# Shifting the SBUF start addresses of a two-layer network's matmul operands by 64 bytes

## The chip, the cores and the metric

The kernel runs on one core of one Trainium2 chip. The metric is the device time of one execution in microseconds, the median of three runs. "Moving" is the operand that streams through TensorE, "stationary" the one that a weight load (LDWEIGHTS) places in the array before the matmul. All sizes and offsets are per SBUF partition; an offset means start address modulo 128 bytes.

## The reference

```python
def reference(...):
    x = attention in chunks of 64 over q, k, v            # (8, 8, 576, 64)
    x = _moe_ref(x.transpose(...).reshape(8, 576, 512), ...)  # causal attention of 4 experts, 2 chosen
    return _moe2_ref(x, g_ln, w_ch1, w_ch2)

def _moe2_ref(x, g_ln, w_ch1, w_ch2):                     # "the second network"
    mu = np.mean(x, axis=-1, keepdims=True)
    var = np.mean((x - mu) ** 2, axis=-1, keepdims=True)
    xn = (x - mu) / np.sqrt(var + 1e-06) * g_ln
    ch = np.maximum(xn @ w_ch1, 0.0) @ w_ch2              # 512 -> 2048 -> 512 for 4608 rows
    return (x + ch).astype(np.float32)
```

## The kernel before, in words

The first 447 us are the two attentions; the change leaves their matmuls alone. After them the second network runs as two matrix products, one after the other, each by a Strassen-like scheme of seven products on quarter blocks. Every fp32 operand is split into a high and a low part, so that each product takes three matmuls (stationary high with moving low, low with high, high with high). All 6048 matmuls have a 128x128 stationary and a 128x256 moving operand of type float32r, and each comes with its own weight load.

**First product** (`prod1`, L864, 3024 matmuls, from `group1_steps`). The moving operand is the normalised input, seven tiles `x7_1` to `x7_7` in pool `sx`, made anew for each of nine row blocks j. The stationary operand is a weight chunk `w1u0` to `w1u7`. The loop over `seq` takes four steps d for each j; step d uses chunks 2d and 2d+1. A step issues seven groups of twelve matmuls in the order (1, n), (7, n), (3, n-1), (6, n), (4, n-1), (2, n), (5, n): groups 3 and 4 belong to the step before and use its chunks. Groups 1, 3, 6 and 5 write the bank `bb`, groups 2, 4 and 7 the pair `ad`. In steps 1 and 2 of each j but the last, eight transposes of the next block (`norm`, L802) stand between groups 4 and 2.

**Second product** (`group2`, L1132, 3024 matmuls). Here the weights `w2u1` to `w2u7` move, and the hidden activations are stationary: `his` and `los`, halves of 4 KB that `take()` deals out of a free list of slots left by the first product (`x7_*`, `xc`, `raw64`, `cv`, `cw`, named `hx7_*`, `hxc`, `hraw64`, `hcv`, `hcw` there) and of seven new ones (`n0` to `n6`, later `hn*`). `product` issues low, high, high for each block.

Where a tile lies is set by the pools: they are stacked from both ends of SBUF, in the order in which they are opened, so a tile's offset follows from the sizes of those before it. In the program before, the offsets of the second network's operands are these two, 64 bytes apart:

```
operand                                        before   after
x7_1 to x7_7          moving, first product        96      32
w1u0 to w1u3          stationary, first            96      96
w1u4 to w1u7          stationary, first            32      96
w2u1, w2u2, w2u5-7    moving, second product       96      32
w2u3, w2u4            moving, second               32      32
hraw64, hcv, hcw, n*, hn*   stationary, second     32      96
hx7_*                 stationary, second           96      96
hxc (two buffers)     stationary, second       96, 32      96

pairs moving/stationary, matmuls   96/96  96/32  32/32  32/96
first product, before               1512   1512      -      -
second product, before               704   1456    488    376
both products, after                   -      -      -   6048
```

The prediction speaks of *same* pairs (96/96 and 32/32) and *crossed* pairs (96/32 and 32/96). The functions that the diff touches:

Of the kernel before, what the change touches and what calls it, by code (L numbers as in the profile page):

```python
# [7 lines left out]
F32 = mybir.dt.float32  # L8
F32R = mybir.dt.float32r
# [13 lines left out]
def tile_kernel(ctx, tc, dims, qkt, vt, wqt, wkt, wvt, wo, g_ln, w_ch1, w_ch2, out):  # L23
    nc = tc.nc
    B, H, S, D = dims
    E, HD, DM = wo.shape
# [13 lines left out]
    VW = NV + E  # L40
# [13 lines left out]

    def f32(ap):
        return ap.bitcast(F32)

    ident = const.tile([128, 128], F32)
    nc.gpsimd.memset(ident, 0.0)
# [7 lines left out]
    sc = ctx.enter_context(tc.tile_pool(name="sc", bufs=1, side="right"))  # L67
    se = early.enter_context(tc.tile_pool(name="se", bufs=1, side="right"))
# [64 lines left out]
    def part_of(n):  # L133
        c, half = n[0], int(n[1])
        if c == "o":
            return woh[:, half, :], wol[:, half, :], wo[2 * half:2 * half + 2].rearrange("e d n -> (e d) n"), None
        hi, lo, src, sc = SRC[c]
        fs = slice(half * 2, half * 2 + 2)
        return hi[:, fs, :], lo[:, fs, :], src[:, fs, :], sc

    held = {}
    PARTS = [c + h for c in "kqvo" for h in "01"]

    def weight_load(n):
        src = part_of(n)[2]
        c, half = n[0], int(n[1])
        if c not in held:
            held[c] = se.tile([128, 4 * VW], F32, name="wraw") if c == "q" else sc.tile([128, 4 * VW], F32, name="xc", bufs=2)
        raw = held[c][:, half * 2 * VW:half * 2 * VW + src.size() // 128]
        if half:  # L150
            held.pop(c)
        if c != "o":
            raw = raw.rearrange("p (a b) -> p a b", a=2)
        nc.sync.dma_start(raw, src)
        raws[n] = raw
# [8 lines left out]
    def weight_low(n, eng):  # L164
        hi, lo, _, sc = part_of(n)
        if sc is None:
            eng.tensor_tensor(lo, raws.pop(n), f32(hi), OP.subtract)
        else:
            eng.scalar_tensor_tensor(lo, raws.pop(n), sc, f32(hi), OP.mult, OP.subtract)
# [50 lines left out]
    def chunk_split(g, acc):  # L220
        gi, j = divmod(g, GT)
        if j == 0:
            groups[gi] = (sp_.tile([128, KF, GW], F32R, name="xTh", bufs=2), sp_.tile([128, KF, GW], F32R, name="xTl", bufs=2))
        cs = slice(j * 128, (j + 1) * 128)
        xh, xl = (x[:, :, cs].rearrange("p f (c i) -> p f c i", c=2) for x in groups[gi])
        src = acc.rearrange("p c f i -> p f c i")
        return (lambda: nc.scalar.activation(xh, src, AF.Copy)), (lambda: nc.vector.tensor_tensor(xl, src, f32(xh), OP.subtract))
# [471 lines left out]
    def start_up(op):  # L699
        c, n = op[0], op[1:]  # L700
        if n in PARTS:
            if c == "c":
                weight_load(n)
            elif c == "h":
                weight_high(n)
            else:
                weight_low(n, nc.vector if c == "l" else nc.gpsimd)
        elif c == "P":
            if not projs:
                projs.append(proj_group(0))  # L710
            high, low = next(projs[0])
            highs.append(high)
            lows.append(low)
        elif c == "a":
            highs.pop(0)()
        elif c == "v":
            lows.pop(0)()
        elif c == "G":
            next(projs.pop(0))
            step(gates[0])  # L720
        elif c == "N":
            chunk_shift(int(n), paired.pop(int(n)))
        elif c == "K":
            paired[n, "k"] = chunk_turn(int(n))
        elif c == "k":
            paired.pop((n, "k"))()
        elif c in "HX":
            paired[int(n)].pop(0)()
        else:
            prologue[c](int(n))  # L730
# [8 lines left out]
    w1u = {}  # L739

    def new_w1(pool, c):
        w1u[c] = pool.tile([128, 2, 2, 7, 128], F32R, name=f"w1u{c}", tag=f"u{c}")

    def load_w1(c):
        nc.sync.dma_start(f32(w1u[c][:, :, 1]), w1d[c])
# [18 lines left out]
    x7, tsum, xt = {}, {}, {}  # L764
# [4 lines left out]


    def norm(j, half):
        xc = sc.tile([128, 4 * VW], F32, name="xc", bufs=2)[:, :2 * DM].rearrange("p (a b) -> p a b", a=2)
        nc.sync.dma_start(xc, xs[2 * j + half])
        yield
        mv = sc.tile([128, 2, 2], F32, name="mv", bufs=2)
        for i in range(2):
            st = sc.tile([128, 6], F32, name="st", bufs=2)
            nc.vector.bn_stats(st, xc[:, i])
            nc.vector.bn_aggr(mv[:, i, :], st)
        ve = sc.tile([128, 2], F32, name="ve", bufs=2)  # L780
        sd = sc.tile([128, 2], F32, name="sd", bufs=2)
        rs = sc.tile([128, 2], F32, name="rs", bufs=2)
        nw = sc.tile([128, 2], F32, name="nw", bufs=2)
        nc.vector.tensor_scalar(ve, mv[:, :, 1], 1e-6, None, OP.add)
        nc.scalar.activation(sd, ve, AF.Sqrt)
        yield
        nc.vector.reciprocal(rs, sd)
        nc.vector.tensor_tensor(nw, rs, rs, OP.mult)
        nc.vector.tensor_tensor(nw, nw, ve, OP.mult)
        nc.vector.tensor_scalar(nw, nw, -0.5, 1.5, OP.mult, OP.add)  # L790
        nc.vector.tensor_tensor(rs, rs, nw, OP.mult)
        for i in range(2):
            nc.vector.tensor_scalar(xc[:, i], xc[:, i], mv[:, i, 0:1], rs[:, i:i + 1], OP.subtract, OP.mult)
        yield
        if half == 0:
            xt[j] = sx.tile([128, 4, KF, 256], F32, name="xt")
        t = xt[j][:, half]
        across.add((j, half))
        tp = pss.tile([128, 2, KF, 128], F32, name="tp2", tag="ps2")
        for i in range(2):  # L800
            for f in range(KF):
                nc.tensor.transpose(tp[:, i, f, :], xc[:, i, f * 128:(f + 1) * 128], ident)  # L802
        nc.scalar.activation(t.rearrange("p f (i n) -> p f i n", i=2), tp.rearrange("p i f n -> p f i n"), AF.Copy)
        yield
# [16 lines left out]
            yield  # L821

    def operand_high(j, i):
        t = x7[j, i] = sx.tile([128, 2, 2, 256], F32R, name=f"x7_{i}")
        nc.scalar.activation(t[:, 0], tsum[i], AF.Copy)  # L825

    def operand_low(j, i, eng=nc.vector):
# [4 lines left out]
    def operand(j, i):  # L832
        operand_high(j, i)
        operand_low(j, i)
# [3 lines left out]
    def begin(op):  # L838
        c, n = op[0], int(op[1])
        eng = nc.gpsimd if op[-1] == "P" else nc.vector  # L840
        if c == "i":
            step(started.setdefault(n, norm(0, n)))
        elif c == "u":
            difference(0, n, eng)
        elif c == "h":
            operand_high(0, n)
        elif c == "l":
            operand_low(0, n, eng)
        elif c == "g":
            w1_high(n, int(op[2]))  # L850
        elif c == "m":
            w1_low(n, int(op[2]), eng)
# [63 lines left out]
    def first_weights():  # L916
        nonlocal w1p, sq
        mids.close()
        w1p = ctx.enter_context(tc.tile_pool(name="w1p", bufs=1, side="right", reuse_waits="tile"))
        for c in range(2):  # L920
            new_w1(w1p, c)
            load_w1(c)
        sq = ctx.enter_context(tc.tile_pool(name="sq", bufs=1, side="right", reuse_waits="tile"))
# [12 lines left out]
    sx = ctx.enter_context(tc.tile_pool(name="sx", bufs=1, side="right", reuse_waits="tile"))  # L936
# [7 lines left out]
    for c in range(2, 4):  # L944
        new_w1(w1r, c)
        load_w1(c)
# [3 lines left out]

    w1q = ctx.enter_context(tc.tile_pool(name="w1q", bufs=1, reuse_waits="tile"))
    cx = ctx.enter_context(tc.tile_pool(name="cx", bufs=1, reuse_waits="tile"))
    low = ExitStack()
    w1z = low.enter_context(tc.tile_pool(name="w1z", bufs=1, reuse_waits="tile"))
    for c in range(4, NC):
        pool = w1q if c < 6 else w1z
        new_w1(pool, c)
        load_w1(c)
        if c == 5:
            released.append(True)  # L960
            while kept:
                store(*kept.pop(0))
# [19 lines left out]
    POOLS = {f"x7_{i}": sx for i in range(1, 8)}  # L982
# [16 lines left out]
    def take():  # L999
        t = free.pop(0)  # L1000
        if t in fresh:
            return t, fresh.pop(t)
        if t == "xc":
            return t, sc.tile([128, 4 * VW], F32R, name="hxc", tag=t, bufs=2)[:, :1024].rearrange("p (a b) -> p a b", a=4)
        return t, POOLS[t].tile([128, 4, 256], F32R, name="h" + t, tag=t)

    def give(h):
        free.append(h[0])
# [178 lines left out]
    for n, (j, d) in enumerate(seq):  # L1187
        if d == 0 and j + 1 < NB:
            nrm = [norm(j + 1, 0), norm(j + 1, 1), sums(j + 1)]
            step(nrm[0])  # L1190
            step(nrm[1])
# [40 lines left out]
    n = len(seq) - 1  # L1232
# [10 lines left out]
    for i in range(7):  # L1243
        t = f"n{i}"
# [94 lines left out]
```

## Time and profile before

| what | value |
|---|---|
| median of three runs | 1183.58 us (1183.41 to 1184.11) |
| span of the profiled execution | 1181.6 us |
| the runs' median less that span (start and end) | 1.98 us |
| PE busy | 1167.0 us, 99% |
| weight loads busy | 1120.1 us, 95% |
| DVE, ACT, POOL busy | 75%, 49%, 23% |
| chain of work that ended last | PE 93%, DVE 4% |

The profiled execution's own time is not among the three; its span lies 1.98 us under their median. A busy PE says little here: matmuls are pipelined, a row of one lasts some 280 ns, and the next one starts less than half of that later. What a matmul costs is the distance from its start to the next start, and that is read from the timeline: its rows merge matmuls of one line with the same names, so the distance between two rows' starts, divided by the matmuls of the first, is the cost of one.

### The profile page before, as it was taken

To read this page: it belongs to the slowest core of one execution; us is meant where nothing else is said; L and a number is where in the kernel's file an instruction comes from. 1 tells how busy PE (TensorE), PEld (TensorE's weight loads), DVE (VectorE), ACT (ScalarE), POOL (GpSimd) and SP (SyncE) were. 2 spreads that over 40 slices of the span, in tenths; PEclk is the share of its full clock that TensorE was granted. 3 is DMA by queue.
4 is the path that set the end of the run, shared out by engine and by line. 5 is a ranking of instruction groups with operands and counts; after the bars stand their busy time and mean duration, and the time that the engine had idled before them with its cause. 6 is when DMAs were issued, how large, how long until landed. Compare 5 with 4: busy or idle time off the path is not lost.

```text
span 1181.6 us, 29119 instructions
## 1 busy us (share of the span) xinstructions
PE 1167.0 (99%) x11840; PEld 1120.1 (95%) x11840; DVE 891.7 (75%) x1830; ACT 579.0 (49%) x1099; POOL 276.9 (23%) x490
## 2 busy tenths in 40 slices
PE   8999999999999999999999999999999999999998
PEld 7889989998998879999999999999999999999998
DVE  6888797879888686975776686457998777877783
ACT  4665665656666585533443333346543334333340
POOL 4544545544553450221211211110000000000000
PEclk9999999999999999999999999999999999999999
DMA  8345343334331136755555545559855454545421
GB/s 310 109 142 178 124 148 131 132 134 150 107 131 62 69 102 241 225 187 173 170 184 185 178 164 176 175 168 320 306 178 170 159 163 153 169 155 167 166 86 45
DMA packets 95509, 191.69 MB, mean 162 GB/s; under 512 B 8592, under 2 KB 41360, under 8 KB 94480
## 3 DMA queue, kind: packets, MB, share of 16 engines
q1 hardware_dynamic: 95376, 189.83, 48.6%
q8 instruction: 93, 1.52, 0.5%
q14 instruction: 40, 0.33, 0.1%
HBM read 118.50 MB, written 71.30 MB: 161 GB/s over the span
## 4 chain that ended last, share of the span: by engine, by line
PE 93%; DVE 4%; ACT 1%; issue 1%; DMA 0%; POOL 0%; DVEq 0%; ACTq 0%; POOLq 0%
PE bb L864 17%; PE bb L1132 17%; PE ad L864 13%; PE ad L1132 11%; PE pp L274 8%; PE pv L301 4%; PE oa_ps L458 4%; PE y_ps L468 4%; PE tp L439 4%; PE sp L388 4%; PE sx_ps L182 1%; PE tp L802 1%; PE pT_ps L208 1%; PE sx_ps L218 1%; DVE P L406 1%; ACT P L411 1%
## 5 line engine op out<-in xcount | busy, mean ns | idle before, releaser
L864 PE MATMUL bb<-x,w1u 128*128 128x256 f32 x1728 | 215.8, 280 | 0.0
L864 PEld LDWEIGHTS bb<-x,w1u 128*128 128x128 f32 x1728 | 209.1, 190 | 0.1
L864 PE MATMUL ad<-x,w1u 128*128 128x256 f32 x1296 | 168.7, 282 | 0.0
L864 PEld LDWEIGHTS ad<-x,w1u 128*128 128x128 f32 x1296 | 159.1, 190 | 0.3 <-issue 0.2
L1132 PE MATMUL bb<-w2u,hn 128*128 128x256 f32 x712 | 121.5, 280 | 0.3 <-DVE hn L1056 0.3
L1132 PEld LDWEIGHTS bb<-w2u,hn 128*128 128x128 f32 x712 | 102.3, 189 | 0.5 <-DVE hn L1056 0.5
L428 POOL TENSOR_SCALAR P<-P,l 128x128 f32<-128x128 f32 (+8 forms) x144 | 88.7, 633 | 42.3 <-DVE l L421 37.6
L1132 PE MATMUL bb<-w2u,hx 128*128 128x256 f32 x464 | 94.5, 282 | 0.0
L411 ACT ACTIVATE P<-P,nm 128x128 f32<-128x128 f32 (+8 forms) x144 | 86.9, 607 | 14.4 <-DVE nm L406 14.4
L513 POOL TENSOR_TENSOR cv<-cv 128x512 f32<-128x512 f32 x16 | 27.1, 1696 | 231.1 <-DVE cv L509 231.1
L1132 PE MATMUL ad<-w2u,hn 128*128 128x256 f32 x472 | 81.1, 280 | 0.0
L543 POOL TENSOR_TENSOR cw<-cw 128x128 f32<-128x128 f32 x128 | 64.3, 522 | 60.7 <-issue 41.1
L1132 PEld LDWEIGHTS bb<-w2u,hx 128*128 128x128 f32 x464 | 74.1, 189 | 0.0
L1132 PE MATMUL ad<-w2u,hx 128*128 128x256 f32 x416 | 73.2, 281 | 0.0
L1132 PEld LDWEIGHTS ad<-w2u,hn 128*128 128x128 f32 x472 | 68.6, 188 | 0.0
L406 DVE CUSTOM_DVE_ANT_0 P<-sp,mcaus 128x128 f32<-128x128 f32 (+7 forms) x128 | 60.2, 517 | 8.4 <-PE sp L388 8.0
L829 DVE TENSOR_TENSOR x<-xt,x 128x512 fp32r<-128x512 f32 x61 | 49.8, 817 | 16.9 <-ACT x L825 16.9
L1132 PEld LDWEIGHTS ad<-w2u,hx 128*128 128x128 f32 x416 | 61.0, 189 | 0.0
L458 PE MATMUL oa_ps<-pTa,vg 128*64 128x128 f32 x928 | 59.6, 278 | 0.5 <-DVE pTa L443 0.3
L202 POOL TENSOR_TENSOR pc<-pc,lc 128x512 f32<-128x512 f32 x35 | 37.5, 1072 | 85.8 <-DVE lc L198 62.9
L439 PE MATMUL tp<-ident,P 128*128 128x128 f32 x464 | 57.4, 274 | 0.0
L458 PEld LDWEIGHTS oa_ps<-pTa,vg 128*64 128x64 f32 x928 | 50.7, 138 | 4.7 <-issue 1.1
(353 smaller groups left out, 2821.4 us busy)
## 6 DMA issues: line engine op xcount, KB each, us to landing
qk<-in_qk SPq DMA_DIRECT2D x35, 512.0 KB, 4.2
raw<-in_w_ch SPq DMA_DIRECT2D x32, 512.0 KB, 3.9
hx<-hd SPq DMA_DIRECT2D x28, 512.0 KB, 4.2
hn<-hd SPq DMA_DIRECT2D x24, 512.0 KB, 4.3
vb<-in_v SPq DMA_DIRECT2D x36, 256.0 KB, 4.3
xs<-y SPq DMA_DIRECT2D x36, 256.0 KB, 2.2
xc<-xs SPq DMA_DIRECT2D x18, 512.0 KB, 4.4
hd<-p SPq DMA_DIRECT2D x36, 256.0 KB, 4.3
```

The source lines that it names most:

```text
L274: nc.tensor.matmul(pp, a[:, f, ws], b_[:, f, :], start=(f == 0 and n == 0), stop=(f == KF - 1 and n == 2))
L301: nc.tensor.matmul(pv, a[:, f, cs], b_[:, f, :], start=(f == 0 and n == 0), stop=(f == KF - 1 and n == 2))
L388: nc.tensor.matmul(sv[:, si, :cn], x[r, ep, qc], y[r, ep, c0:c0 + cn], start=first, stop=last)
L406: nc.vector.tensor_tensor_reduce(dst, src, mk, -1.0, -3.0 * NEG, OP.add, OP.min, nm[:, e2:e2 + 1])
L411: nc.scalar.activation(pe, pe, AF.Exp, bias=nm[:, e2:e2 + 1], scale=-1.0, accum_out=l[:, e2:e2 + 1])
L428: nc.gpsimd.tensor_scalar(pe, pe, sums_[g][:, ep, e2:e2 + 1], 1.0, OP.mult, OP.mult)
L439: nc.tensor.transpose(tp[:, i, :], P[ep][e2][:, kt * 128:(kt + 1) * 128], ident)
L458: nc.tensor.matmul(o_ps[e2 * HD:(e2 + 1) * HD, ep, :], vg[:, gk % GT, e * HD:(e + 1) * HD], pT[:, e * n + kt, :], start=(kt == 0), stop=(k ...
L543: nc.gpsimd.tensor_tensor(w[:, o, :], w[:, x, :], w[:, y, :], op)
L829: eng.tensor_tensor(t[:, 1], tsum[i], f32(t[:, 0]), OP.subtract)
L864: nc.tensor.matmul(out[:, p], w[:, kt, a, WI[i], :], x[:, b_, kt, :], start=(start and p == 0 and kt == 0 and q == 0), stop=False, skip_gr ...
L1132: ins = nc.tensor.matmul(out, x[:, c, ts], w2u[i][:, w, half * 4 + c, :], start=begin and q == 0, stop=False, skip_group_check=True)
```

## The change

It puts every moving operand of the second network at offset 32 and every stationary one at 96. Three tools do it: a gap tile of 64 bytes in a pool (`gap`), a tile made longer (`xc` rounded up to whole 128 bytes, an `x7` slot 128 bytes longer than its data), and a view that starts 64 bytes into its tile (`SHIFT`, 16 elements: `w1u0` to `w1u5`, and the slots of `sx` when they hold activations).

```diff
+    LINE = 128
+    MOVING, STILL = 32, 96
+    SHIFT = (STILL - MOVING) // 4
+    XC = -(-4 * VW * 4 // LINE) * LINE // 4
+    SLOT = 1024 + LINE // 4
+
+    def gap(pool, size, name):
+        pool.tile([128, size // 4], F32, name=name)
...
     def new_w1(pool, c):
-        w1u[c] = pool.tile([128, 2, 2, 7, 128], F32R, name=f"w1u{c}", tag=f"u{c}")
+        at = 0 if c > 5 else SHIFT
+        t = pool.tile([128, at + 3584], F32R, name=f"w1u{c}", tag=f"u{c}")
+        w1u[c] = t[:, at:].rearrange("p (k s i n) -> p k s i n", k=2, s=2, i=7)
...
     def norm(j, half):
-        xc = sc.tile([128, 4 * VW], F32, name="xc", bufs=2)[:, :2 * DM].rearrange("p (a b) -> p a b", a=2)
+        xc = sc.tile([128, XC], F32, name="xc", bufs=2)[:, :2 * DM].rearrange("p (a b) -> p a b", a=2)
...
     def operand_high(j, i):
-        t = x7[j, i] = sx.tile([128, 2, 2, 256], F32R, name=f"x7_{i}")
+        t = x7[j, i] = sx.tile([128, SLOT], F32R, name=f"x7_{i}")[:, :1024].rearrange("p (a k t) -> p a k t", a=2, k=2)
+        if (j, i) == (0, 5):
+            gap(sx, STILL - MOVING, "xgap")
...
     cx = ctx.enter_context(tc.tile_pool(name="cx", bufs=1, reuse_waits="tile"))
+    gap(cx, STILL - MOVING, "cgap")
...
-        return t, POOLS[t].tile([128, 4, 256], F32R, name="h" + t, tag=t)
+        at = SHIFT if POOLS[t] is sx else 0
+        h = POOLS[t].tile([128, at + 1024], F32R, name="h" + t, tag=t)
+        return t, h[:, at:].rearrange("p (a b) -> p a b", a=4)
```

No instruction is added, removed or moved on any engine: each one's sequence is the same in both programs, operation by operation. All semaphore waits are the same but one: the DVE subtraction that makes the low part of the first `x7_7` (`operand_low`, L829) waits for one transfer more of a DMA queue, the load of a `vb` tile of the first attention (L118).

## Rows read from the trace of the kernel before

**Rows 1.** The page: span, busy time of TensorE, chain that ended last.
```profile
span 1181.6 us, 29119 instructions
...
PE 1167.0 (99%) x11840; PEld 1120.1 (95%) x11840; DVE 891.7 (75%) x1830; ACT 579.0 (49%) x1099; POOL 276.9 (23%) x490
...
PE 93%; DVE 4%; ACT 1%; issue 1%; DMA 0%; POOL 0%; DVEq 0%; ACTq 0%; POOLq 0%
```

**Rows 2.** Second network: window, length; PE busy (matmuls); granted clock; DMA share; GB/s.
```profile
447.90:1178.50 730.60, 730.28 (x6223) 1.00 0.55 178
```

**Rows 3.** Waits of PE from 447 us on: total us, times, longest.
```profile
PE bb L1132 <- DVE hn L1056: 0.3, 1, 0.3
```

**Rows 4.** PE's timeline, first product: start us, us, engine, line, operation, names, shapes, count.
```profile
461.99 3.04 PE L864 MATMUL bb<-x,w1u 128*128 128x256 f32 x24
464.87 1.60 PE L864 MATMUL ad<-x,w1u 128*128 128x256 f32 x12
466.31 1.04 PE L802 MATMUL tp<-ident,xc 128*128 128x128 f32 x8
467.11 1.68 PE L864 MATMUL ad<-x,w1u 128*128 128x256 f32 x12
...
471.42 1.52 PE L864 MATMUL ad<-x,w1u 128*128 128x256 f32 x12
472.78 2.96 PE L864 MATMUL bb<-x,w1u 128*128 128x256 f32 x24
...
477.02 1.04 PE L802 MATMUL tp<-ident,xc 128*128 128x128 f32 x8
477.81 1.66 PE L864 MATMUL ad<-x,w1u 128*128 128x256 f32 x12
479.31 2.99 PE L864 MATMUL bb<-x,w1u 128*128 128x256 f32 x24
...
489.20 3.00 PE L864 MATMUL bb<-x,w1u 128*128 128x256 f32 x24
...
508.51 1.68 PE L864 MATMUL ad<-x,w1u 128*128 128x256 f32 x12
```

**Rows 5.** PE's timeline, end of the first product.
```profile
808.77 2.88 PE L864 MATMUL bb<-x,w1u 128*128 128x256 f32 x24
...
818.29 1.52 PE L864 MATMUL bb<-x,w1u 128*128 128x256 f32 x12
```

**Rows 6.** PE's timeline, start of the second product, up to its one wait.
```profile
827.91 5.60 PE L1132 MATMUL aa<-w2u,n 128*128 128x256 f32 x48
833.35 0.28 PE L1132 MATMUL ad<-w2u,hcv 128*128 128x256 f32 x1
...
841.95 0.62 PE L1132 MATMUL bb<-w2u,hn 128*128 128x256 f32 x3 [0.27 <-DVE hn L1056]
```

**Rows 7.** PE's timeline, second product: w2u3 with hn, then w2u4 with hx.
```profile
864.67 3.04 PE L1132 MATMUL bb<-w2u,hn 128*128 128x256 f32 x24
867.54 0.28 PE L1132 MATMUL ad<-w2u,hx 128*128 128x256 f32 x1
...
870.36 2.99 PE L1132 MATMUL ad<-w2u,hx 128*128 128x256 f32 x24
873.19 0.28 PE L1132 MATMUL bb<-w2u,hn 128*128 128x256 f32 x1
```

**Rows 8.** PE's timeline: another run with hx (two of w2u7, then w2u4).
```profile
1104.68 3.25 PE L1132 MATMUL ad<-w2u,hx 128*128 128x256 f32 x27
1107.77 0.40 PE L1132 MATMUL ad<-w2u,hn 128*128 128x256 f32 x2
```

**Rows 9.** PE's timeline: the last matmuls.
```profile
1176.85 1.60 PE L1132 MATMUL dt<-w2u,hn 128*128 128x256 f32 x12
```

**Rows 10.** Loads of vb (first and last issue); DVE's subtractions that make low parts.
```profile
L118 SPq DMA_DIRECT2D vb<-in_v x36: 327/364/1107, 3.6 to 337.8; - x36
...
L829 DVE TENSOR_TENSOR x<-xt,x x61: 670/693/1787, 432.7 to 788.4; 128x512 fp32r<-128x512 f32 x61
```

More of the change, by code (lines that the diff above doesn't have):

```diff
@@ L147, in weight_load @@
         if c not in held:
-            held[c] = se.tile([128, 4 * VW], F32, name="wraw") if c == "q" else sc.tile([128, 4 * VW], F32, name="xc", bufs=2)
+            held[c] = se.tile([128, 4 * VW], F32, name="wraw") if c == "q" else sc.tile([128, XC], F32, name="xc", bufs=2)
         raw = held[c][:, half * 2 * VW:half * 2 * VW + src.size() // 128]
@@ L1003, in take @@
         if t == "xc":
-            return t, sc.tile([128, 4 * VW], F32R, name="hxc", tag=t, bufs=2)[:, :1024].rearrange("p (a b) -> p a b", a=4)
-        return t, POOLS[t].tile([128, 4, 256], F32R, name="h" + t, tag=t)
+            return t, sc.tile([128, XC], F32R, name="hxc", tag=t, bufs=2)[:, :1024].rearrange("p (a b) -> p a b", a=4)
+        at = SHIFT if POOLS[t] is sx else 0
+        h = POOLS[t].tile([128, at + 1024], F32R, name="h" + t, tag=t)
+        return t, h[:, at:].rearrange("p (a b) -> p a b", a=4)
     def give(h):
```

## Prediction, made before the changed kernel ran

> **What bounds the kernel now.** I read the page first: TensorE is busy 99% of a span of 1181.6 us and makes up 93% of the chain that ended last [rows 1]. The change touches only the stretch from 447.9 us to the last matmul, so I took that window next. TensorE is busy there for 730.28 of 730.60 us at a granted clock of 1.00 (2.4 GHz) [rows 2], and in the whole of it the view of its waits has one entry, of 0.3 us [rows 3]. So the second network is a row of 6048 matmuls that stand shoulder to shoulder, and the change is worth whatever it does to the distance from one start to the next, 6048 times: one nanosecond of it is 6 us. The timeline gives that distance, and it isn't one number.
>
> - *Same pairs* (96/96 in the terms of the table of offsets). The row at 464.87 holds twelve matmuls with chunks w1u0 and w1u1, and the next row starts at 466.31: 1.44 us / 12 = 120.0 ns [rows 4]. The other same pair, 32/32, does likewise: 24 matmuls of w2u3 with hn from 864.67 to 867.54, 119.6 ns each [rows 7].
> - *Crossed pairs at 113.* The row at 471.42 is group 7 of step 2, with w1u4 and w1u5 (96/32): 1.36 us / 12 = 113.3 ns [rows 4]. At the end of the first product 84 matmuls from 808.77 to 818.29 take 113.3 ns each [rows 5], and 48 of the second product from 827.91 to 833.35 also 113.3 [rows 6].
> - *Crossed pairs at 118.* The same chunks, the same code, one step later: from 479.31 to 489.20 there are 84 matmuls with w1u4 to w1u7, 9.89 us, 117.7 ns each [rows 4].
>
> So a crossed pair keeps one of two paces, 4.4 ns apart ("at 113" and "at 118" below), and holds it as long as nothing else comes between. What comes before decides. After eight transposes the crossed stretch that begins at 477.81 is at 118 [rows 4]. The eight blocks j that have such transposes before a crossed stretch all do this. After a stretch of same pairs it is at 113: the row at 471.42 follows twelve same pairs, and there is no transpose ahead of the stretch at 808.77 [rows 4, 5]. A wait acts like the transposes: the second product starts at 113, comes to its one pause, 0.27 us at 841.95 [rows 6], and is near 118 on the mean from there on (below).
>
> **The change, part by part.** It makes every pair 32/96, a crossed pair that the kernel before has 376 times. The longest pure stretches of it are 24 long. The one at 870.36 takes 2.83 us / 24 = 117.9 ns [rows 7]. One of them holds 113: 27 matmuls from 1104.68, two of them still 96/96, take 114.4 ns each [rows 8]. So 32/96 knows both paces too, and the question is which one the kernel settles in when *all* pairs are crossed. No row of before shows that. From both sides: 113.3 ns at best, 120.0 ns if all go like same pairs. I take 117.7, because in the changed kernel what now brings a crossed stretch to 113, the same pairs ahead of it, is gone, while the transposes and the wait that bring it to 118 stay. Then:
>
> - First product, the 120 matmuls ahead of 467.11, all same pairs (3024 less the two items that follow): from 120.0 to 117.7 ns, 120 x -2.3 = -0.3 us.
> - First product, eight periods of 336 matmuls like the one from 467.11 to 508.51 [rows 4]: 168 same pairs gain 2.3 ns, 108 crossed pairs at 118 (from 477.81 to the next same pairs) stay, and 60 at 113 (groups 1, 7 and 6 of step 2; 3 and 4 of step 0) lose 4.4 ns: -0.386 + 0.264 = -0.12 us each, together -1.0 us.
> - First product, last 216 matmuls, where block j = 8 has no transposes: 48 same pairs -0.1 us, 168 crossed ones at 113 [rows 5] +0.7 us.
> - Second product up to the wait: 144 pairs at 113 [rows 6] +0.6 us, 24 mixed ones nothing.
> - Second product after the wait: 2844 matmuls from 841.95 to 1176.85 [rows 6, 9], 334.90 us, or 117.76 ns each; without the 0.11 us that the first one takes longer, 117.72. That mixture of all four pairs already costs what a crossed stretch at 118 does: 0.0 us.
>
> Sum: -0.3 - 1.0 - 0.1 + 0.7 + 0.6 = -0.1 us. Taking 117.8 for 117.7, within the reading of these rows, adds 0.6 us, so I take the middle, +0.2. **What the same pairs give, the crossed pairs at 113 pay back.** The sum is made on the profiled execution: 1181.6 + 0.2 = 1181.8 us of span, and with the 1.98 us by which the median of the runs stands above that span, 1183.8 us.
>
> The rest is free. The gaps and longer tiles are never read or written. The one wait that grows, DVE's first x7_7 subtraction, is for a vb load: the last of all 36 vb loads is issued at 337.8 us, and the first L829 subtraction runs at 432.7 [rows 10], so the load has landed some 90 us before. DVE, ACT and the queues get the same instructions in the same order, and their slack stays as it is, since TensorE's pace does.
>
> A rule of the Trainium skill speaks against any effect at all. Its page "TensorE: Matmul & The Clock Gate", section "Step-by-step: what each phase is for", says that TensorE reads the moving operand and the weights through two independent ports, so that loading the next weights takes no read bandwidth from the running matmul. By that rule offsets could not matter, and the sum would be 0, 1183.6 us. The trace disagrees with it here, 120.0 against 113.3 ns for two groups of one instruction that differ in one offset [rows 4].
>
> **The rivals.**
>
> 1. *All at 113.* That pace may be the one that a pure crossed stream falls into, and 118 an after-effect of offset 96 in the moving operand. For it: 32/96 held it once [rows 8], and 84 in a row hold 113.3 ns [rows 5]. Against it: the other long stretches of 32/96 are at 118 [rows 7], and so are the crossed pairs after the transposes, in eight of eight blocks. Price: 1512 same pairs x -6.7 = -10.1 us, 864 crossed ones at 118 of the first product x -4.4 = -3.8, 2844 of the second x -4.4 = -12.5: 1183.6 - 26.4 = **1157.2 us**.
> 2. *Part of it.* One product turns to 113 and the other doesn't, since the wait at 841.95 starts the second one afresh; or some breaks do. Only the first: -13.9 + 0.6 = 1170.3 us; only the second: 1183.6 - 12.5 - 0.7 = 1170.4 us; single blocks anywhere from there to 1181.
> 3. *Slower: a stream that starts after a break locks at 120.0 ns.* Rows at offset 32 in the moving operand show 119.6 ns when the stationary one also lies at 32 [rows 7]. If what counts is the moving operand's offset with whatever came before it, 32/96 after a transpose takes that pace, and no other kind of pair comes to end it. Decided by the first stretch after the transposes: 120.0 there is this case. Price: 1512 crossed pairs of the first product (864 x 2.3 + 648 x 6.7 = 6.3 us), 144 x 6.7 + 2844 x 2.3 = 7.5 us in the second: **1197.4 us**. Against it: 32/96 runs at 117.9 right after mixed pairs [rows 7].
> 4. *The offsets do nothing*; the differences come from something else that the rows happen to go along with, such as which tiles are used. 1183.6 us. Against it: the same chunks w1u4 and w1u5 run at 113.3 and at 117.7, so more than tiles counts, and no pure run of theirs is at 120. It is what the rule of the Trainium skill's page "TensorE: Matmul & The Clock Gate" (same section) would have.
>
> **How the numbers follow.** A measurement of this kernel can tell some 0.2% from no change, 2.4 us. Forecast, 117.7 ns throughout: 0.54. All at 113: 0.14. Part of it: 0.20. Slower: 0.08. Nothing: 0.04. Same is the forecast and "nothing", 0.58; faster 0.34; slower 0.08. The range leaves out the case of all at 113 and most of the slower one, 0.2 together: from 1167, a little below one product at 113, to 1187, where a fifth of the pairs would have gone to 120. The forecast's own range is 1181.5 to 1185.5 (117.4 to 118.0 ns over 6048).
>
> **What would show it.** In the timeline after, rows of 24 matmuls should last 2.99 us from one end of the second network to the other (3.04 is 120.0 ns, 2.88 is 113.3), rows of twelve start 1.41 us apart, and 808.77's counterpart should have lost its pace of 113.3. If the row after the transposes shows 2.88, the forecast is wrong from the step "I take 117.7" on. If single rows differ, offsets above 128 bytes count too, which I left out.

## The result and the profile after

The changed kernel takes 1170.01 us (median of four runs, 1169.12 to 1171.09) against 1183.84 us of the kernel before in the same session (1183.41 to 1186.21): a ratio of 0.988, 95% interval 0.9866 to 0.9894, so 12.5 to 15.9 us faster. The forecast was 1183.8 us, no change.

The page after; the three lines answer to [rows 1]:

```profile
span 1168.5 us, 29119 instructions
...
PE 1151.4 (99%) x11840; PEld 1104.7 (95%) x11840; DVE 891.6 (76%) x1830; ACT 578.8 (50%) x1099; POOL 276.4 (24%) x490
```

Same instructions, same busy share of 99%: the busy share alone would tell nothing. The windows split the second network at the first matmul of the second product (columns: window, length, busy time of PE, PEld, DVE, ACT, POOL with their instructions, granted clock, DMA share, GB/s). Before:

```profile
447.90:819.65 371.75, 371.75 (x3176) 371.11 (x3174) 250.32 (x491) 156.44 (x262) 61.52 (x81) 1.00 0.59 191
819.65:1178.30 358.65, 358.38 (x3050) 358.13 (x3048) 279.32 (x278) 137.34 (x139) 0.00 (x0) 1.00 0.51 165
```

After:

```profile
447.66:817.75 370.09, 369.61 (x3175) 368.80 (x3174) 249.58 (x491) 156.09 (x261) 61.42 (x81) 1.00 0.60 192
817.75:1165.20 347.45, 346.89 (x3050) 346.42 (x3048) 278.78 (x278) 137.66 (x139) 0.00 (x0) 1.00 0.53 170
```

The granted clock is 1.00 in all four. The first product gave 1.7 us, **the second 11.2 us**. In it the stream starts at 118, has a short break at the place of the wait in [rows 6] (0.29 us from the start at 840.25 to the next one, at 840.54), and turns to 113 there (PE's timeline; columns as in [rows 4]):

```profile
826.23 5.82 PE L1148 MATMUL aa<-w2u,n 128*128 128x256 f32 x48
831.88 0.28 PE L1148 MATMUL ad<-w2u,hcv 128*128 128x256 f32 x1
...
840.54 3.00 PE L1148 MATMUL bb<-w2u,hn 128*128 128x256 f32 x24
843.38 2.88 PE L1148 MATMUL bb<-w2u,hn 128*128 128x256 f32 x24
...
862.42 2.88 PE L1148 MATMUL bb<-w2u,hn 128*128 128x256 f32 x24
865.14 0.28 PE L1148 MATMUL ad<-w2u,hx 128*128 128x256 f32 x1
...
867.86 2.88 PE L1148 MATMUL ad<-w2u,hx 128*128 128x256 f32 x24
871.30 2.88 PE L1148 MATMUL bb<-w2u,hn 128*128 128x256 f32 x23 [0.55 <-DVE hn L1093]
...
1163.80 1.52 PE L1148 MATMUL dt<-w2u,hn 128*128 128x256 f32 x12
```

From 826.23 it is 5.65 us / 48 = 117.7 ns. The 24 matmuls from 840.54 take 2.84 us, the slow start after the break included. From 862.42 it is 2.72 / 24 = 113.3. The 2844 matmuls from 840.54 to 1163.80 take 323.26 us; their counterparts in [rows 6, 9] took 334.90. At 871.30 there is now a wait that the kernel before did not have (0.55 us): TensorE has overtaken DVE there. The stream is at 113 before that wait and behind it.

The first product stays a mixture. Its timeline, answering to [rows 4]:

```profile
465.57 1.03 PE L813 MATMUL tp<-ident,xc 128*128 128x128 f32 x8
466.36 1.66 PE L877 MATMUL ad<-x,w1u 128*128 128x256 f32 x12
467.86 2.89 PE L877 MATMUL bb<-x,w1u 128*128 128x256 f32 x24
470.58 1.57 PE L877 MATMUL ad<-x,w1u 128*128 128x256 f32 x12
472.00 2.94 PE L877 MATMUL bb<-x,w1u 128*128 128x256 f32 x24
474.78 1.52 PE L877 MATMUL ad<-x,w1u 128*128 128x256 f32 x12
476.14 1.04 PE L813 MATMUL tp<-ident,xc 128*128 128x128 f32 x8
476.93 1.66 PE L877 MATMUL ad<-x,w1u 128*128 128x256 f32 x12
478.43 2.99 PE L877 MATMUL bb<-x,w1u 128*128 128x256 f32 x24
481.25 1.58 PE L877 MATMUL ad<-x,w1u 128*128 128x256 f32 x12
```

24 matmuls from 467.86 go at 113.3, the next twelve at 118.3, those from 474.78 at 113.3 again; after the second transposes everything is at 118. No row is at 120.0 any more.

To read the experiments one more number is needed: the **place**, the start address modulo 256. The change gives every operand one offset modulo 128, but not one place. Moving: x7_1, 6, 4, 5 and all w2u lie at 160, x7_7, 2, 3 at 32. Stationary: 224, but the slots hx7_7, hx7_2, hx7_3 and one of the two hxc at 96 (640 of the second product's 3024).

### The profile page after: what moved, and what is told of

It reads as the page before. It is cut to its first block, busy times and chain, and to the rows that moved or that the text cites. A ratio compares the mean times of both kernels' runs of the same rounds, so it can differ in the third digit from the quotient of the medians.

```text
span 1168.5 us, 29119 instructions
## 1 busy us (share of the span) xinstructions
PE 1151.4 (99%) x11840; PEld 1104.7 (95%) x11840; DVE 891.6 (76%) x1830; ACT 578.8 (50%) x1099; POOL 276.4 (24%) x490
## 4 chain that ended last, share of the span: by engine, by line
PE 53%; DVE 3%; DMA 1%; issue 0%; ACT 0%; SPq 0%; DVEq 0%; ACTq 0%
PE bb L877 15%; PE bb L1148 15%; PE ad L877 11%; PE ad L1148 10%; DMA hx<-hd 1%; PE tp L813 1%; PE dt L1148 0%; DVE hn L1093 0%; DVE w2u L1011 0%; DVE xr L1176 0%; DVE hxc L1068 0%; DVE hx L1057 0%; ACT hn L1069 0%; DVE x L842 0%; DVE hx L1064 0%
## 5 line engine op out<-in xcount | busy, mean ns | idle before, releaser
L1148 PE MATMUL bb<-w2u,hn 128*128 128x256 f32 x712 | 118.4, 276 | 0.6 <-DVE hn L1093 0.6
L1148 PE MATMUL bb<-w2u,hx 128*128 128x256 f32 x464 | 91.6, 276 | 0.0
L448 PEld LDWEIGHTS tp<-ident,P 128*128 128x128 f32 x464 | 51.4, 141 | 3.7 <-issue 2.0
```

Source lines behind the costliest of these rows:

```text
L448: nc.tensor.transpose(tp[:, i, :], P[ep][e2][:, kt * 128:(kt + 1) * 128], ident)
L1148: ins = nc.tensor.matmul(out, x[:, c, ts], w2u[i][:, w, half * 4 + c, :], start=begin and q == 0, stop=False, skip_group_check=True)
```

## The experiments

All times are beside the kernel before on the same chip (1183.4 to 1184.1 us median per session). Means are of the distances from start to start that are under 150 ns, in the one run of each kernel that was traced. Diffs are against the changed kernel; `SLOT`, `XC`, `gap` as in the change. Where a kernel was run once, the number is that one run. Of the theories in the quoted expectations, A says that only offsets modulo 128 count; the others are told where they come up.

### Is it the distance of 64 bytes?

`swap` puts all moving operands at 96 and all stationary ones at 32; `even` at 64 and 0; `same` puts all 6048 pairs at 32/32; `even_slots` makes the x7 slots 128 bytes longer, so that all seven lie at place 160.

```diff
# swap                                   (even: 224, 32 and [8:1032])
+    gap(sx, STILL - MOVING + 192, "xgap");  gap(w1q, 64, "lgap");  hxc view [16:1040]
# same
+    SHIFT = 0;  gap(cx, 2 * LINE, "cgap");  hxc view [16:1040]
# even_slots
+    SLOT = 1024 + 2 * LINE // 4;  gap(sx, STILL - MOVING + 128, "xgap")
```

> Every operand of the second network lies 64 bytes further on than in the changed kernel: moving at 96, stationary at 32, all pairs 96/32. Theory A (only the distance of 64 bytes between the two counts): the same as the changed kernel, 1170 us; second product at 113.3 ns from its pause on, first product near 117.7 ns. Theory B (moving at 32 is what let the pause bring the second product to 113; at 96 a pause leaves it at 118, as the one pause of the kernel before did): second product at 117.7 ns throughout, 1182 to 1184 us. Theory C (the 13 us came from somewhere else than the pause): no number, but the second product would then change its pace at another place than a pause.

> Every operand 32 bytes further on than in the changed kernel: moving at 64, stationary at 0, still 64 bytes apart, but both on a multiple of 64. Theory A (only the distance counts): 1170 us, same paces at the same places. Theory D (a start that is not a multiple of 64 costs one more piece of 64 bytes per operand, 17 for 1024 bytes, and 113.3 is that price): distances of 109 to 111 ns become possible, 10 to 25 us less than the changed kernel, 1145 to 1160 us.

> All pairs 32/32: the stationary operands lie at 32, like the moving ones. If a same pair costs 120.0 ns wherever it stands alone: 6048 times 120.0, some 13 us over the kernel before, 1195 to 1198 us, and 27 us over the changed kernel. If 120.0 belonged to 96/96 alone: 118 or less, 1170 to 1184 us.

> As the changed kernel, but the seven x7 slots stand 4352 bytes apart, not 4224, so all seven start 160 bytes past a multiple of 256 (changed kernel: four of them, 1, 6, 4 and 5, at 160 and three, 7, 2 and 3, at 32). In the changed kernel the first product goes from 113 to 118 whenever the moving tile changes from one at 160 to one at 32, and comes back in steps 0 and 1 when it changes the other way. Theory E (the change of the moving operand's offset by 128 is what switches the pace): no switch inside a step any more; after the transposes the first product stays at 118 until a pause, so it gets slower by some 477 x 4.4 ns = 2 us: 1172 us. Theory F (160 itself is the good offset, 32 the bad one): the first product comes to 113 right after the transposes and stays, 2500 x 4.4 = 11 us less: 1159 us.

| kernel | time, us | first product, mean ns | second, mean ns |
|---|---|---|---|
| before | 1183.84 | 117.85 | 117.52 |
| changed | 1170.01 | 117.10 | 113.58 |
| swap | 1169.68 | 117.09 | 113.34 |
| even | 1167.46 | 116.10 | 113.70 |
| same | 1193.02 | 119.26 | 119.46 |
| even_slots | 1164.71 | 114.38 | 113.35 |

Nothing in `swap` depends on which operand has which offset, and multiples of 64 are nothing special: no distance of 110 ns or less appeared. Same pairs throughout cost 119.4 ns on the mean and 9 us more than before, somewhat less than expected. But `even_slots` shows that offsets modulo 128 are not all: it moves only the place of three x7 slots, and the first product loses 2.7 ns per matmul. Its time lies between those of theories E and F. Group by group (twelve matmuls or more on one x7 tile, no break between): in `even_slots` all 181 changes of tile that come at 113 leave it at 113, and all 48 that come at 118 leave it at 118.

### Do same pairs hurt their neighbours?

```diff
# one_same
+        at = SHIFT if POOLS[t] is sx and t != "x7_6" else 0
```

> The changed kernel with one of its slots, hx7_6 (144 of the second product's stationary operands, from 854 to 1094 us), put back to offset 32, so that these pairs are the same kind again (32/32). Theory C (contagion: a same pair also moves the crossed pairs after it to 118, and that is why the kernel before was at 118 in the second product): from the first use of hx7_6 on, crossed stretches are at 118 at least until the next event that brings 113; second product up to 12 us longer, total 1174 to 1182 us. Theory O (a same pair costs only itself): 144 x 6.7 ns = 1.0 us, total 1171 us, all stretches without hx7_6 at 113.3.

It took 1174.0 us. The timeline of `one_same`, second product:

```profile
849.68 5.60 PE L1148 MATMUL bb<-w2u,hn 128*128 128x256 f32 x48
855.12 0.28 PE L1148 MATMUL ad<-w2u,hcw 128*128 128x256 f32 x1
...
857.94 2.99 PE L1148 MATMUL ad<-w2u,hn 128*128 128x256 f32 x24
860.77 0.28 PE L1148 MATMUL bb<-w2u,hn 128*128 128x256 f32 x1
```

The 48 matmuls ahead of hx7_6 take 113.3 ns, the 24 crossed ones behind it (857.94) 117.9. The second product's mean is 114.60 ns, 3.1 us more than in the changed kernel; the 144 same pairs by themselves explain 1.0. So here same pairs drag the crossed pairs behind them to 118. It is contagion, but short of the 12 us of its extreme: several blocks later the stream is back at 113.

### What sets the pace of a crossed stream?

`far128` lifts the left-hand stationary operands to place 96. `no_transposes` leaves the transposes of blocks 1 to 8 out. `pause` adds to `even_slots` a matmul that must wait for ScalarE.

```diff
# far128
+    gap(cx, STILL - MOVING + LINE, "cgap")
# no_transposes: if j > 0, instead of tp and the transposes
+            nc.scalar.activation(t[...], xc[...], AF.Copy)
# pause: after the copy out of tp, if j > 0
+            nc.tensor.matmul(tp[:, 0, 0:2, :], w1u[0][:, 0, 0, 0, :], x7[j - 1, 1][:, 0, 0, :], ...)
```

> The changed kernel with the left-hand stationary operands (hraw64, hcv, hcw, n*, hn*, w1u6, w1u7) 128 bytes higher: offset mod 128 as in the change (96), but mod 256 at 96 instead of 224, so that most pairs of the second product are 128 bytes further apart. Theory D256 (what a crossed stream keeps after the pause near 840 us is set by the distance mod 256, as the kernel before with 224/160 went to 118 there and the changed one with 160/224 to 113): the pause leads to 118, the second product keeps about 117.7 ns for long, total 1175 to 1182 us. Theory A (only offsets mod 128 and the event count): as the changed kernel, pause to 113, total 1168.5 to 1171.5 us.

> The changed kernel without the transposes of blocks j = 1 to 8 (128 of the 144 transposes are left out, the normalised rows are copied untransposed, so the first product computes with other numbers). If the transposes are what holds the first product at 118 (the step of the prediction): after the first steps it goes at 113.3 throughout, mean under 114, the first product about 10 us shorter than its 375.6 us on top of the transposes' own 13 us. If it is the moving tiles' places 128 bytes apart (x7_1, 6, 4, 5 at 160 mod 256, x7_7, 2, 3 at 32) that turn the pace inside the steps: the mean stays at 116.5 to 117.7 and only the transposes' own time, some 11 to 13 us, is gone.

> The changed kernel with the x7 slots 4352 bytes apart (all seven at 160 mod 256, which took 1164.7 us), and after each eight transposes of blocks j = 1 to 8 one more matmul of the usual form whose output is not used and which has to wait until ScalarE has read the transposes: 16 pauses of 1 to 2 us ahead of the stream. If a pause brings a crossed stream to 113: all 16 stretches after the pause are at 113.3 and none starts at 118 (without the pauses 8 of the 16 did), first-product mean 113.5 ns or less outside the pauses, total 1164.7 + 16 x (1 to 2) - 2 = 1178 to 1195 us. If what sets the pace is where the operands lie, not the pause: the first stretch after the pause is at 118 in about half of the 16, as without pauses.

`far128`: 1168.25 us. It ran at 118 past 840 us, so that no wait arose there, and turned to 113 near 853, in the first block that alternates hcw (place 96) with hx7_6 (224). What was asked of the wait stayed unanswered.

`no_transposes`: 1154.55 us, first product 115.61 ns, 1552 distances at 116 to 119 and 1450 at 111 to 115: between the two expectations, since the transposes do cost some pace, but half of the stream is at 118 without them. There all 63 changes from a tile at place 160 to one at 32 that came at 113 left it at 118, and 65 of the 71 back brought 113. So a good part of what holds the changed kernel's first product at 118 is its own tiles, which lie at two places.

`pause`: 1168.13 us. The extra matmul was issued some ten matmuls late and hardly had to wait (0.57 us once), so the time is less than expected, but it breaks the stream. After 14 of the 16 breaks the pace is 113, after two 118. In the unforced waits of all traces up to here, both occur too. So a break can end either way; what decides it, no run shows.

### One place for all

`plus64`: all pairs at places 160/224. `minus64`: all at 32/224, the same offsets modulo 128. `plus96` and `plus32`: as `plus64`, stationary operands 32 bytes up or down.

```diff
# plus64
+    SLOT = 1024 + 2 * LINE // 4;  gap(sx, STILL - MOVING + 128, "xgap")
+    XC = -(-4 * VW * 4 // (2 * LINE)) * (2 * LINE) // 4;  hxc view [32:1056]
# minus64
+    SLOT and XC as above, no xgap;  hxc view [32:1056];  gap(w1q, LINE, "lgap")
+    gap(cx, STILL - MOVING + LINE, "cgap");  at = SHIFT + LINE // 4 for w1u0 to w1u5 and hx7
```

> All 6048 pairs 32/96 as in the change, and moreover all at one place mod 256: moving 160, stationary 224, so that the stationary operand always lies 64 bytes above the moving one mod 256. Theory D256 (a disturbed crossed stream falls to 113 where the distance stationary less moving is +64 mod 256, and to 118 where it is -64): nothing but the transposes can bring 118, no tile change does; first product at 114.5 ns or less, second at 113.3 to 113.4 throughout; total 1162 to 1165.5 us. Theory A (only mod 128 counts, the rest is chance of the events): like the changed kernel, 1166 to 1171 us.

> All 6048 pairs 32/96 as in the change, but all at moving 32, stationary 224 mod 256: the stationary operand lies 64 bytes below the moving one mod 256 (-64). Theory D256: transposes and pauses bring 118 and nothing brings 113 back; both products at 117.5 to 117.9 ns, total 1181 to 1185 us, which is what the prediction gave for the change. Theory A (only mod 128 counts): like the changed kernel, 1166 to 1171 us.

> As the kernel with all pairs at +64, but every stationary operand 32 bytes higher: moving 160, stationary 0 mod 256, distance +96. If the pace goes by the distance in a smooth way between 120.0 at 0 and at 128 bytes and 113.3 at 64: between 114 and 118 ns, total 1170 to 1185 us. If anything that isn't 0 or 128 will do: 113.3 ns and a total of 1162 to 1166 us.

> As the kernel with all pairs at +64, but every stationary operand 32 bytes lower: moving 160, stationary 192 mod 256, distance +32. If the pace goes by the distance in a smooth way: as at +96, 114 to 118 ns, total 1170 to 1185 us. If anything that isn't 0 or 128 will do: 113.3 ns, 1162 to 1166 us. Below 113 would be a third pace that no trace so far has shown.

`plus64` refuted the theory D256: its ten runs fell into heaps, four at 1169.6 to 1171.8 us, five at 1182.2 to 1184.0, one at 1178.3. The profiled one (1183.37) shows what the upper heap is, by its window and timeline:

```profile
841.86:1178.30 336.44, 336.44 (x2856) 336.44 (x2856) 1.00 0.49 154
```

```profile
838.40 2.92 PE L1148 MATMUL bb<-w2u,hn 128*128 128x256 f32 x24
841.86 5.92 PE L1148 MATMUL bb<-w2u,hn 128*128 128x256 f32 x48 [0.55 <-DVE hn L1072]
847.62 0.28 PE L1148 MATMUL bb<-w2u,hcv 128*128 128x256 f32 x1
```

After the one wait the pace is 118, and it stays so over 2856 matmuls to the end, 117.8 ns each. Here, where all pairs lie at one place, nothing turned it. 2844 x 4.4 ns = 12.5 us is about the distance between the heaps, whose means lie 12.6 us apart; no run of the lower heap was traced. `minus64` took 1183.39 us, 117.79 and 117.78 ns. `plus96` took 1186.41 us and `plus32` 1186.81, both above what either expectation gave, with a third or more of the distances at 120 and over: 32 bytes off the distance of 64, the pace goes part of the way to that of same pairs.

### A place apart, as a turner

`turn` is `plus64` with the slots x7_2, x7_3 and x7_7 at place 96 when they hold activations, 464 pairs as in the changed kernel. `minus64_turn` does the same to `minus64`. `turn_xc` also shifts the rows that the transposes take as stationary operand to place 224.

```diff
# turn                                  (minus64_turn: + (0 if t in (...) else LINE // 4))
+        at = SHIFT + (LINE // 4 if t in ("x7_2", "x7_3", "x7_7") else 0) if POOLS[t] is sx else 0
# turn_xc, in norm
+        xc = ...[:, 32:32 + 2 * DM].rearrange("p (a b) -> p a b", a=2)
```

> The kernel with x7 slots 4352 bytes apart once more, now in many runs. It differs from the one with all pairs at one place mod 256 (whose runs fell into two heaps, 1169.6 to 1171.8 and 1178 to 1184 us) in the places of the two xc buffers alone: one lies at 96 mod 256, the other at 224, so 176 pairs of the second product have a stationary operand 128 bytes off the others. Theory M (a break throws a crossed stream to 113 or 118 by chance; it stays there until a pair at another place mod 256 comes, which turns 118 to 113): one heap, all runs 1163 to 1167 us. Theory U (unlucky chance at the pause decides the second product in every kernel alike): two heaps 12 us apart here too.

> The kernel with all pairs at one place mod 256, but the slots x7_2, x7_3 and x7_7 hold activations 128 bytes higher (96 instead of 224 mod 256; 464 of the second product's stationary operands, the same three slots as in the changed kernel). One view offset, no address of any other tile moves. Theory M: the second heap of runs (1178 to 1184 us) is gone, because the first block in which one of these slots is the single one of three, w2u4 with hx7_3 near 867 us, turns 118 to 113 whatever the pause at 841 us did; all runs 1169 to 1172 us, the first product at 117.5 as without it. Theory U: two heaps as before, median anywhere between 1170 and 1184 us.

> As the kernel with the three slots 128 bytes higher, and besides the normalised rows that the transposes take as stationary operand lie 128 bytes higher in both xc buffers (224 mod 256 instead of 96). Theory X (where the transposes' own stationary operand lies decides what they leave behind: in the kernel with 4352-byte slots the transposes from the buffer at 224 left 113 and those from the one at 96 left 118, 8 of 8 each): all 16 stretches after transposes go at 113, first product 113.3 to 113.8 ns, total 1157 to 1161 us. If it is only which half of the block the transposes belong to: 8 of 16 at 118, first product 114.4 ns, total 1160 to 1164 us. If the xc place doesn't matter: all 16 at 118 as in the kernel without, total 1169 to 1172 us.

> The kernel with all pairs at moving 32, stationary 224 mod 256 once more, now in many runs. It has the change's offsets mod 128 and no pair at another place. Theory M: nothing brings its second product back from 118, so runs at or near 1183 us are there; one or more at about 1170 us may be, if the pause lets it fall to 113 by chance, as with all pairs at 160/224. If -64 always leads to 118: one heap at 1182 to 1185 us.

> As that kernel, but the slots x7_2, x7_3 and x7_7 hold activations 128 bytes lower (96 instead of 224 mod 256; 464 of the second product's stationary operands). Theory M: whatever the pause does, a block in which one of these slots is the single one of three turns 118 to 113 near 867 us, and it stays; second product 113.3 to 114 ns, total 1169 to 1172.5 us in all runs, the first product at 117.8 as without. If the turning works only where the other pairs are at +64: no change, 1182 to 1185 us.

| kernel | median us (runs) | all runs | ratio to before, 95% |
|---|---|---|---|
| plus64 | 1180.26 (10) | 1169.6 to 1184.0 | 0.9908 to 0.9976 |
| turn | 1171.40 (4) | 1170.0 to 1173.0 | 0.9885 to 0.9914 |
| minus64_again | 1183.97 (10) | 1182.1 to 1185.1 | 0.9990 to 1.0008 |
| minus64_turn | 1172.27 (4) | 1171.5 to 1172.7 | 0.9886 to 0.9919 |
| even_slots_again | 1164.96 (4) | 1164.0 to 1166.5 | 0.9833 to 0.9865 |
| turn_xc | **1160.36** (4) | 1159.6 to 1163.4 | 0.9796 to 0.9825 |

Theory M fits all of them: with one view offset on three slots, the upper heap doesn't appear in the four runs of `turn`, and `minus64_turn` takes 11.7 us less than a kernel that had been at 1182 us or more in ten runs of ten. `minus64_turn` is the stronger evidence: four of the ten runs of `plus64` lay in the lower heap without any turner. The profile of `turn` happened to catch it at work:

```profile
868.22 2.88 PE L1148 MATMUL ad<-w2u,hx 128*128 128x256 f32 x24
870.93 3.10 PE L1148 MATMUL bb<-w2u,hn 128*128 128x256 f32 x24
873.87 0.28 PE L1148 MATMUL bb<-w2u,hx 128*128 128x256 f32 x1
873.99 0.40 PE L1148 MATMUL bb<-w2u,hcw 128*128 128x256 f32 x2
...
875.93 0.28 PE L1148 MATMUL bb<-w2u,hx 128*128 128x256 f32 x1
876.04 0.39 PE L1148 MATMUL bb<-w2u,hcw 128*128 128x256 f32 x2
876.27 0.28 PE L1148 MATMUL bb<-w2u,hx 128*128 128x256 f32 x1
876.38 0.39 PE L1148 MATMUL bb<-w2u,hcw 128*128 128x256 f32 x2
876.61 1.64 PE L1148 MATMUL ad<-w2u,hn 128*128 128x256 f32 x13
```

It comes at 113 (2.71 us / 24 from 868.22), is thrown to 118 at 870.93 (2.94 us: the first matmul 0.1 us longer, the rest at 118), and the block of hx7_2 (place 96) with hcw (224) from 873.87 on brings it back: its last triple takes 0.34 us, 113.3 each. In `minus64_turn` the turning came at 861.66, with hn0 and hx7_2, earlier than the block that the expectation named, and held to the end (second product 113.83 ns). In one block `one_same` shows the limit: hn0 with hx7_2 at 860.77 did not turn it, hx7_3 with hxc at 866.45 did.

The changed kernel's own layout turns a stream too. In `even`, where every operand lies as in the changed kernel but 32 bytes further on, a break at 834.09 takes the second product from 113 to 118, and a wait of 0.46 us at 837.64 leaves it there. The block from 863.21 on, hx7_3 with hxc, brings it back:

```profile
860.38 2.99 PE L1149 MATMUL bb<-w2u,hn 128*128 128x256 f32 x24
863.21 0.28 PE L1149 MATMUL ad<-w2u,hx 128*128 128x256 f32 x1
...
865.95 2.88 PE L1149 MATMUL ad<-w2u,hx 128*128 128x256 f32 x24
868.67 1.52 PE L1149 MATMUL bb<-w2u,hn 128*128 128x256 f32 x12
```

It is 2.83 us / 24 = 117.9 ns ahead of the block and 2.72 / 24 = 113.3 behind it.

`turn_xc` bears out the other half, that the place of the transposes' own operand counts. After the transposes, in `plus64`, both xc buffers at place 96:

```profile
464.91 1.03 PE L813 MATMUL tp<-ident,xc 128*128 128x128 f32 x8
465.70 1.66 PE L877 MATMUL ad<-x,w1u 128*128 128x256 f32 x12
467.20 2.99 PE L877 MATMUL bb<-x,w1u 128*128 128x256 f32 x24
```

and in `turn_xc`, both at 224:

```profile
465.19 1.04 PE L813 MATMUL tp<-ident,xc 128*128 128x128 f32 x8
465.99 1.62 PE L877 MATMUL ad<-x,w1u 128*128 128x256 f32 x12
467.44 2.88 PE L877 MATMUL bb<-x,w1u 128*128 128x256 f32 x24
```

In `plus64` and `turn` all 16 stretches after transposes are at 118, in `turn_xc` 15 of 16 at 113, in `even_slots_again` (one buffer at 96, one at 224) 8 and 8. With other places it is less strict: in `minus64_again`, both buffers at 96 too, two of the 16 are at 113. The first product falls from 117.33 ns in `turn` to 113.91. `turn_xc` beats both kernels: 23 us under the one before, and 9.7 under the change (whose time is from another session).

## Why the prediction was wrong

- **What bounds the kernel** was right: TensorE's pace, and nothing else, moved the time. The two paces, the 120.0 of same pairs and the readings of the rows before all came back in the runs.
- **The step that failed** is "I take 117.7, because ... the transposes and the wait that bring it to 118 stay", with its last term, "Second product after the wait: ... 0.0 us". That term measured -11.6 us (334.90 to 323.26). The premise behind it was "A wait acts like the transposes", read from the kernel's one wait. Breaks end either way: the wait at 841.95 left 118 before, the break at 840.54 took the stream from 118 to 113 after, and in `plus64` the heaps suggest that the same wait of one program ends now so, now so. The other half of the premise, that same pairs ahead bring a crossed stretch to 113, does not hold in the second product either: after the wait of the kernel before, twelve pure crossed stretches of 20 or more matmuls follow same pairs, and eight of them are at 118, four at 113; in `one_same` the crossed pairs behind the same ones went to 118. And 118 isn't kept for good: the text had no place for what turns a stream back, the pairs at another place modulo 256. It named the gap itself ("offsets above 128 bytes count too, which I left out").
- The forecast's own number is what the chip gives where a stream stays at 118: `minus64_again`, same offsets modulo 128, one place for all, 1183.97 us, ratio 0.9990 to 1.0008. The second product of its traced run has no wait at all and is at 118 from its first matmul to its last.
- **Where the gain comes from.** In the kernel before, same pairs sit all over the second product. They run near 120 themselves, and the crossed ones among them are mostly at 118: of 1380 distances of crossed pairs after the wait, 875 are at 116 to 119, 382 at 111 to 115 (pairs with hxc left out). That the same pairs are what keeps them there is argued from `one_same`. The change takes the same pairs away. In its traced run the break at 840.54 then brought 113 by itself, and the stream stayed there. That its slots at place 96 would mend a break that ends at 118 is argued from `even` and `turn`. The first alone isn't enough: without same pairs, but without turners too, it is 1184 us or two heaps.
- **First product**: forecast -0.3 - 1.0 - 0.1 + 0.7 = -0.7 us, measured -1.7 with the 0.5 us wait at 498.86. That it is only 1 us off is in part luck; the reason given, transposes alone, was half of it: they do leave 118, but the x7 tiles' two places, which the prediction left out, bring it there too (`no_transposes`).
- The +0.6 us of the second product up to the wait came true: 117.7 ns from 826.23 instead of 113.3.
- **Rivals.** The first (all at 113, 1157.2 us) didn't occur in the changed kernel; `turn_xc` comes near it. The second (only the second product at 113, 1170.4 us) is what happened, 0.4 us off. The third, a lock at 120.0, didn't occur. The fourth, that the offsets do nothing, fell: the addresses alone span 1160 to 1193 us in these runs. With it fell what the prediction drew from the rule of the Trainium skill's page "TensorE: Matmul & The Clock Gate", section "Step-by-step: what each phase is for", which says that loading the next weights takes no read bandwidth from the running matmul. Whether read bandwidth is what the addresses cost, no run here shows.

## What to carry to other kernels

Where each matmul brings its own weight load, look at the distance from start to start, not at busy time, and group it by the start addresses of both operands. Keep moving and stationary operands off the same offset modulo 128 (64 bytes apart was best here), check what each break leaves behind, and run such a kernel often: a median over a pace that is thrown anew in each run says little. An address that is better on paper (all pairs alike) can be worse than a mixture that turns a bad pace back.

## What was not expected of the hardware

One kind of matmul, one clock (granted 1.00), and three paces: 113.3, 117.7 and 120.0 ns, by the start addresses of its operands modulo 256 and by what ran before; with 32 or 96 bytes between the operands the distances are spread from 115 to 123 ns. A pace once taken held for 2856 matmuls (336 us) in `plus64`. The place of eight transposes' stationary operand went with the pace of the 84 or more matmuls behind them. A run's time can so be a coin's throw: about 12.5 us between heaps of one and the same program.

Open: what in the chip holds a pace, what decides how a break ends, and why the same step between places turns 113 to 118 in the first product (moving tile from 160 to 32) and 118 to 113 in the second (stationary operands mixed). That the changed kernel itself has one heap because of its slots at place 96 is argued from `even`, `turn` and `minus64_turn`; in it the x7 slots lie too close to move them, and it was not tried.
